# Two pairs of heads of batch 1, laid out crossed, share TensorE's 64x64 quadrants

## The chip, the core and the metric

The kernel runs on one core of one Trainium2 chip. A core has TensorE (PE in the profile; PEld is its loading of weights), VectorE (DVE), ScalarE (ACT), GpSimd (POOL, which here mostly issues DMAs) and SyncE (SP, which issues DMAs too). The metric is the device time of one launch in microseconds, the median of several runs.

## The reference

A sliding-window attention feeds a feed-forward layer with a squared ReLU. There are 8 batches, 8 heads, 576 tokens and 64 elements a head.

```python
scores = scale * np.matmul(q, k.transpose(0, 1, 3, 2))
rel = pos[:, None] - pos[None, :]
mask_plain = (rel >= 0) & (rel < window)
mask_dil = (rel >= 0) & (rel < window * dilation) & (rel % dilation == 0)
masks = np.stack([mask_plain if h < H // 2 else mask_dil for h in range(H)], axis=0)
...
attn = attn / (np.sum(attn, axis=-1, keepdims=True) + 1e-09)
return np.matmul(attn, v).astype(np.float32)
...
h = np.maximum(x @ w_in, 0.0)
return (h * h @ w_out).astype(np.float32)
```

The window is 32, the dilation 4. The first four heads ("plain") look at the last 32 tokens, the other four ("dilated") at every fourth of the last 128. The attention's output, 4608 tokens by 512, goes through w_in (512 by 2048) and w_out (2048 by 512).

## The kernel before, in words

**The feed-forward layer** makes up most of the work. It runs in tiles of 256 tokens (four of them) and then of 512. A tile is a list of groups, small closures of TensorE work: `mm1` multiplies by w_in (line 937 of the profile) into a PSUM tile `pf`, which ScalarE (line 950) and VectorE (line 951) turn into h2T, and `g2` multiplies by w_out (line 979), whose result ScalarE copies out (line 985).

**The attention** is put between these groups. Its heads come in pairs e = 0 to 3, of which 0 and 1 are plain, 2 and 3 dilated. The two heads of a pair (hl = 0, 1) lie in the lower and the upper 64 partitions. Batch 0 has code of its own, batches 0 and 1 are worked in two parts of 256 and 320 tokens, and from batch 2 on `quadrants` (line 661) runs products of 64x64 elements, four at a time, in the four quadrants of TensorE's array.

**Batch 1**, which the change touches, is laid out in block diagonals. K lies in `kbd`, a tile of 128x128 blocks with zeros off the diagonal, and V likewise in `vbd`. So one full 128x128 product does both heads of a pair, and half of the array multiplies by zeros. For a pair and a part the steps are:

- `trans` (line 277) transposes q or k on TensorE, and `halves` copies the result to `qT` or into the blocks of `kbd` (lines 297, 301, 308 and 314), on ScalarE or VectorE.
- `scores` (lines 351 and 357) multiplies keys by queries into a PSUM tile `pa`; ScalarE's exponential (line 361) and VectorE's mask (line 362) give the weights `pt`.
- `pv` multiplies V's blocks by the weights into a tile o (line 414), and a block diagonal of ones by them into a tile d (line 416), the denominators. Then ScalarE takes the logarithm of d (line 418) and the exponential of its negative (line 419), and VectorE multiplies o by that into `xT` (line 429), which is the feed-forward layer's input. The tiles o and d are `po` and `pd`, one buffer each, or two of the four buffers `pf` where the step's code ends in f.

**The order** is written out by hand in the string `PROGRAM`. Its fields, split at the bars, follow one group of the feed-forward layer each, and `step` runs each code: `1o0` is batch 1, `pv` of pair 0, first part; `1p2` is pair 2, second part; `1a3` are the scores of pair 3, first part, `1b0` those of pair 0, second part; q, Q, k and K transpose, and `2t0` and `2t1` do so for batch 2 with a copy out on ScalarE and VectorE (lines 264 and 262). All engines work off their queues in this order. The fields around the two places are

```python
"... | 1o2 | 1a0 1a1 | 1k3 1o0 1o1f | 1a3 1Q0 | 1K0 1o3 | 1Q1 1K1 | 1Q2 | 1b0 | ..."
"... | 1b2 1p0 | 1b1 1V3 1K3 | L3:x | 1p2 1p1f | 1b3 | 2t0 2t1 1p3f | ..."
```

**Crossed.** `crossed(b, e)` says for which pairs the keys of head hl meet the other half, so that head hl's scores come out in the other 64 partitions. Two pairs, one crossed and one not, then use different quadrants of the array. Before the change no pair of batch 1 is crossed. The code `n` in PROGRAM clears the off-diagonal halves of `kbd` ahead of batch 1 (lines 998 and 999). DMAs that load V (`load_v`, line 192, and line 219 for the last block) read from `crossed` which head goes where.

## Time and profile before

| what | value |
|---|---|
| median of 3 runs | 299.42 us (298.89 to 299.48) |
| the profiled execution | 299.32 us, span 297.5 us |
| TensorE busy | 290.4 us, 98% of the span, 3159 products |
| ScalarE, VectorE, GpSimd busy | 192.0, 168.0, 127.6 us |
| products with w_in, line 937 | 128.3 us, 704 |
| products with w_out, line 979 | 129.3 us, 592 |
| granted TensorE clock | 1.00 |

Times in the profile are microseconds from the start of the span. A row of the timeline has the start, the time, the engine, the line, the operation, out<-in, the form and the number of instructions merged in it; in brackets stands how long the engine was idle before, and what released it. A matmul's record runs to its modelled end, some 0.2 us for a small one, while the next one starts much earlier; the pace of products is therefore read from their starts, not from their durations. In a merged row with several widths, the form is that of the first. In the page, a line is followed by the share of the span in brackets and the number of instructions; the chain is that of the work that ended last.

### The profile page before, as it was taken

How to read it: one execution, taken by the hardware profiler on the slowest of the kernel's cores; microseconds unless marked ns; L12 is line 12 of the kernel's file. 1: busy time of each engine (PE TensorE's matmuls, PEld its weight loads, DVE VectorE, ACT ScalarE, POOL GpSimd, SP SyncE). 2: the span in 40 equal slices, each digit the busy share in tenths (PEclk: the TensorE clock that was granted, in tenths of full speed). 3: DMA queues.
4: the chain of work that ended last, by engine and by line, in shares of the span. 5: the costliest groups of instructions: out<-in, count | busy, mean ns of one | idle time of the engine just before them, and what ended most of it. 6: DMA issues, size and time to landing. Idle time of an engine off the chain costs nothing.

```text
span 297.5 us, 7852 instructions
## 1 busy us (share of the span) xinstructions
PE 290.4 (98%) x3159; PEld 166.3 (56%) x3159; DVE 168.0 (56%) x508; ACT 192.0 (65%) x397; POOL 127.6 (43%) x208
## 2 busy tenths in 40 slices
PE   7899999999999999999999999999999999999994
PEld 3589657868755554555455445545554555445443
DVE  2776566967868665686749474957445234004400
ACT  6888568757958665888667667766676567127411
POOL 8579882676584383955783688100000000000000
PEclk9999999999999999999999999999999999999999
DMA  8999999999989999999999499112101200121022
GB/s 126 197 183 215 203 157 223 186 151 169 193 114 185 184 121 190 153 125 175 159 191 151 65 160 186 13 37 73 35 2 36 74 35 0 35 73 35 0 56 88
DMA packets 83124, 35.37 MB, mean 119 GB/s; under 512 B 52624, under 2 KB 78480, under 8 KB 83088
## 3 DMA queue, kind: packets, MB, share of 16 engines
q0 software_dynamic: 48992, 18.40, 54.8%
q1 hardware_dynamic: 33952, 16.38, 27.7%
q8 instruction: 25, 0.41, 0.6%
q10 hardware_dynamic: 144, 0.10, 0.1%
q14 instruction: 11, 0.09, 0.1%
HBM read 37.31 MB, written 9.44 MB: 157 GB/s over the span
## 4 chain that ended last, share of the span: by engine, by line
PE 90%; DMA 5%; ACT 2%; POOL 1%; issue 1%; DVE 1%; ACTq 0%; POOLq 0%
PE pf L937 42%; PE pf L979 40%; DMA w_in<-in_moe_w_in_dram 3%; DMA kb<-in_k_dram 2%; PE po L661 2%; PE pa L661 1%; PE pf L661 1%; POOL qb L171 1%; PE pa L277 1%; PE pd L661 1%; ACT rec L684 0%; ACT pt L698 0%; POOL kb L171 0%; ACT rec L674 0%; PE po L414 0%
## 5 line engine op out<-in xcount | busy, mean ns | idle before, releaser
L937 PE MATMUL pf<-xT,w_in 128*128 128x512 bf16 (+1 forms) x704 | 128.3, 341 | 1.3 <-DMA w_in<-in_moe_w_in_dram 1.3
L979 PE MATMUL pf<-w_out_sb,h2T 128*128 128x512 bf16 (+2 forms) x592 | 129.3, 374 | 0.0
L937 PEld LDWEIGHTS <-w_in 128*128 128x128 bf16 x704 | 77.9, 113 | 48.0 <-DMA w_in<-in_moe_w_in_dram 1.7
L950 ACT ACTIVATE h2T<-pf 128x512 bf16<-128x512 f32 x144 | 83.7, 600 | 29.5 <-PE pf L937 29.3
L951 DVE TENSOR_TENSOR h2T<-h2T 128x512 bf16<-128x512 bf16 x144 | 60.3, 424 | 60.1 <-ACT h2T L950 57.8
L979 PEld LDWEIGHTS <-h2T 128*128 128x128 bf16 x592 | 55.5, 98 | 61.6
L478 POOL DMA_DIRECT2D vbd<-in_v_dram x80 | 43.0, 547 | 24.3 <-DMA qb<-in_q_dram 10.2
L985 ACT COPY osb<-pf 128x512 f32<-128x512 f32 (+1 forms) x34 | 19.5, 573 | 49.7 <-PE pf L979 49.5
L171 POOL DMA_DIRECT2D qb<-in_q_dram x18 | 13.0, 720 | 9.7 <-DMA xx<-qb 7.9
L684 ACT ACTIVATE rec<-rec 128x576 f32<-128x576 f32 x24 | 16.4, 682 | 0.7
L698 ACT ACTIVATE pt<-pa 128x384 bf16<-128x384 f32 (+1 forms) x28 | 12.7, 498 | 6.2 <-DVE xT L689 3.7
L192 POOL DMA_DIRECT2D vbd<-in_v_dram x16 | 10.9, 691 | 9.1 <-DMA kb<-in_k_dram 4.3
L687 DVE TENSOR_TENSOR xT<-po,rec 128x512 bf16<-128x512 f32 x14 | 9.7, 691 | 7.5 <-ACT rec L684 7.2
L171 POOL DMA_DIRECT2D kb<-in_k_dram x18 | 12.7, 706 | 1.7 <-issue 0.7
L465 POOL DMA_DIRECT2D vd<-in_v_dram x20 | 12.0, 616 | 2.9 <-DMA vbd<-in_v_dram 2.9
L470 POOL DMA_DIRECT2D vbd<-in_v_dram x20 | 12.0, 615 | 2.7 <-DMA vbd<-in_v_dram 2.2
L700 DVE TENSOR_TENSOR pt<-pt,mask_n 128x448 bf16<-128x448 bf16 (+1 forms) x20 | 7.1, 373 | 9.5 <-ACT pt L698 9.4
L700 DVE TENSOR_TENSOR pt<-pt,mask_f 128x384 bf16<-128x384 bf16 x24 | 8.4, 355 | 6.0 <-ACT pt L698 5.9
L687 DVE TENSOR_TENSOR xT<-pf,rec 128x512 bf16<-128x512 f32 x10 | 6.9, 691 | 8.5 <-ACT rec L684 8.5
L492 DVE COPY qT<-xx 64x576 bf16<-64x576 bf16 (+1 forms) x30 | 10.8, 360 | 0.6
L661 PEld LDWEIGHTS <-vbd 64*64 64x64 bf16 x288 | 7.6, 107 | 4.2 <-issue 4.2
L698 ACT ACTIVATE pt<-pf 128x448 bf16<-128x448 f32 (+1 forms) x18 | 8.5, 521 | 0.5 <-PE pf L661 0.3
(156 smaller groups left out, 311.8 us busy)
## 6 DMA issues: line engine op xcount, KB each, us to landing
qb<-in_q_dram POOLq DMA_DIRECT2D x7, 320.0 KB, 5.3
kb<-in_k_dram POOLq DMA_DIRECT2D x7, 320.0 KB
vd<-in_v_dram POOLq DMA_DIRECT2D x32, 64.0 KB, 6.1
w_in<-in_moe_w_in_dram POOLq DMA_DIRECT2D x4, 512.0 KB, 8.6
w_out_sb<-in_moe_w_out_dram POOLq DMA_DIRECT2D x4, 512.0 KB, 13.0
out_dram<-osb SPq DMA_DIRECT2D x16, 128.0 KB, 5.3
qb<-in_q_dram POOLq DMA_DIRECT2D x7, 256.0 KB, 7.6
kb<-in_k_dram POOLq DMA_DIRECT2D x7, 256.0 KB
```

The lines of the kernel that those rows point to most:

```text
L171: nc.gpsimd.dma_start(t[0:n, part, hs, :], src[b, hs, t0 : t0 + RES * n, :].rearrange("h (p r) d -> p h (r d)", r=RES))
L478: nc.gpsimd.dma_start(v_rows[b % 2][p0 + 16 * r : p0 + 16 * r + 16, e, :, :], v[b, 2 * e + hl, :, :].rearrange("(i m r) d -> r m i d", r=R ...
L661: nc.tensor.matmul(out, lhs, rhs, start=begin, stop=True, skip_group_check=True)
L684: nc.scalar.activation(rec[:, :], rec[:, :], ACT.Exp, scale=-1.0)
L687: nc.vector.tensor_tensor(out=tok[:, :, 16:M], in0=byr(o[:, :]), in1=byr(rec[:, 0:512]), op=ALU.mult)
L698: nc.scalar.activation(pt, sp[b, e][g][:, 0:n], ACT.Exp, scale=SCALE)
L700: nc.vector.tensor_tensor(out=pt, in0=pt, in1=mask, op=ALU.mult)
L937: nc.tensor.matmul(to, w_in_sb[piece][:, kt, c0 : c0 + 509 : 4], rhs, start=(kt == kts[0] and x == 0), stop=(kt == kts[-1] and x == per - ...
L950: nc.scalar.activation(hv, acc[u][:, :].rearrange("p (x n) -> p x n", x=per), ACT.Relu)
L951: nc.vector.tensor_tensor(out=hv, in0=hv, in1=hv, op=ALU.mult)
L979: nc.tensor.matmul(cur[m][:, c0:c1], h2[:, f, P * m : P * m + P], w_out_sb[:, f, c0:c1], start=(f == 0), stop=(f == NF - 1),)
L985: (nc.vector.tensor_copy if last and part == 1 or tk0 == 3 * NT // 2 else nc.scalar.copy)(osb[:, c0:c1], cur[m][:, c0:c1])
```

## The change

Pair 1 of batch 1 becomes crossed: `crossed` is now 1 for it, `halves` writes its keys into the anti-diagonal of `kbd`, `n` clears the diagonal of that pair's blocks and the off-diagonal of the others (six pieces instead of two), and `load_v` swaps its two heads. `pv` is split: `products` makes the lists of products, yields them, and goes on with logarithm, exponential and the multiplication. `pv` runs one pair as before. The new `pv_two` takes two pairs, cuts each product into the two 64x64 products on its blocks that aren't zero, and issues them in turn from four lists, one a quadrant. The steps `1o0 1o1f` become `1+o01`, and `1p2 1p1f` become `1+p21`. Pairs 0 and 3 in the second part, and 2 and 3 in the first, stay as they were.

The order on ScalarE, GpSimd and SyncE is the same as before, instruction for instruction. On VectorE the only difference are the four more pieces of clearing. On TensorE 16 products in the first place become 32, and 24 in the second become 48.

```diff
-    ... | 1k3 1o0 1o1f | 1a3 1Q0 | ... | 1p2 1p1f | 1b3 | ...
+    ... | 1k3 1+o01 | 1a3 1Q0 | ... | 1+p21 | 1b3 | ...
...
-        return int(b == XB and e in (1, 3) or b >= NATURAL and e == 1 or b >= PAIRED and e == 0)
+        return int(b == 1 and e == 1 or b == XB and e in (1, 3) or b >= NATURAL and e == 1 or b >= PAIRED and e == 0)
...
+            at = sides[hl ^ crossed(b, e)]
...
-                        kbd[rows, e, m0 // 16 : (m0 + n) // 16, rows].rearrange(
+                        kbd[rows, e, m0 // 16 : (m0 + n) // 16, at].rearrange(
...
+    def pv(*args):
+
+        work = products(*args)
+        mms, dms = next(work)
+        for y, items in enumerate((mms, dms)):
+            for x, (to, lhs, rh) in enumerate(items):
+                nc.tensor.matmul(to, lhs, rh, start=(x == 0), stop=(x == len(items) - 1), skip_group_check=True)
+        next(work, None)
+
+    def pv_two(b: int, one, two, part: int):
+
+        works = products(b, one, part), products(b, two, part, ps_f, "pf")
+        todo = {}
+        for e, work in zip((one, two), works):
+            for s, rows in enumerate(sides):
+                cols = sides[s ^ crossed(b, e)]
+                todo[s, cols.start] = items = []
+                lists = next(work) if s == 0 else lists
+                for kind in lists:
+                    for x, (to, lhs, rh) in enumerate(kind):
+                        items.append((to[cols], lhs[rows, rows], rh[rows], x == 0))
+        assert len(todo) == 4
+        while any(todo.values()):
+            for items in todo.values():
+                if items:
+                    to, lhs, rh, begin = items.pop(0)
+                    nc.tensor.matmul(to, lhs, rh, start=begin, stop=True, skip_group_check=True)
+        for work in works:
+            next(work, None)
...
-        for x, (oo, i, rh) in enumerate(mms):
-            nc.tensor.matmul(oo, vb[:, e, i, :], rh, start=(x == 0), stop=(x == len(mms) - 1), skip_group_check=True)
-        for x, (dd, rh) in enumerate(dms):
-            nc.tensor.matmul(dd, ones[:, :], rh, start=(x == 0), stop=(x == len(dms) - 1), skip_group_check=True)
+        yield [(oo, vb[:, e, i, :], rh) for oo, i, rh in mms], [(dd, ones[:, :], rh) for dd, rh in dms]
...
+        if code[0] == "+":
+            pv_two(b, int(code[2]), int(code[3]), int(code[1] == "p"))
+            return
...
-            zero_halves(kbd)
+            for es in (slice(0, 1), slice(2, NE)):
+                zero_halves(kbd[:, es])
+            for rows in sides:
+                nc.vector.memset(kbd[rows, 1, :, rows], 0.0)
```

## The prediction

> **What bounds the kernel now.** I read the page first: busy time of each engine, then the chain that ended last.

> ```profile
> PE 290.4 (98%) x3159; PEld 166.3 (56%) x3159; DVE 168.0 (56%) x508; ACT 192.0 (65%) x397; POOL 127.6 (43%) x208
> ...
> PE 90%; DMA 5%; ACT 2%; POOL 1%; issue 1%; DVE 1%; ACTq 0%; POOLq 0%
> ```

> TensorE is busy for 98% of the span and carries 90% of the chain, at full granted clock. So a product that gets shorter counts, but only if the engine then finds its next input ready. The edit touches batch 1 in two places, and next I read the timeline there, TensorE alone. First place, pairs 0 and 1, first part:

> ```profile
> 47.02 0.32 PE L414 MATMUL po<-pt,vbd 128*128 128x96 bf16 x4
> 47.17 0.32 PE L416 MATMUL pd<-pt,ones 128*128 128x96 bf16 x4
> 47.37 0.32 PE L414 MATMUL pf<-pt,vbd 128*128 128x96 bf16 x4
> 47.52 0.32 PE L416 MATMUL pf<-pt,ones 128*128 128x96 bf16 x4
> 47.68 0.38 PE L979 MATMUL pf<-w_out_sb,h2T 128*128 128x512 bf16 x1
> ```

> Each pair has eight products (three of 96 columns, one of 64, twice), starting 0.04 us apart: 0.31 us a pair. Both pairs start on a wait, which the busy share hides, since a matmul's record overlaps the next. The two masks of VectorE (line 362) run from 46.62 to 47.31 in that timeline, one after the other; pair 0 starts some 0.06 after the first ends, pair 1 at 47.37, 0.06 after the second.

> Second place, pair 2 (dilated) and pair 1, second part; no wait here, both masks are done by 63.92:

> ```profile
> 64.32 0.44 PE L414 MATMUL po<-pt,vbd 128*128 128x32 bf16 x9
> 64.59 0.38 PE L416 MATMUL pd<-pt,ones 128*128 128x320 bf16 x3
> 64.81 0.39 PE L414 MATMUL pf<-pt,vbd 128*128 128x32 bf16 x6
> 65.04 0.39 PE L416 MATMUL pf<-pt,ones 128*128 128x32 bf16 x6
> 65.26 0.38 PE L979 MATMUL pf<-w_out_sb,h2T 128*128 128x512 bf16 x1
> ```

> Behind the first place ScalarE, read alone, has no gap. What it does last here, line 361 at 48.99, is the exponential that pair 3 needs:

> ```profile
> 47.53 0.39 ACT L418 ACTIVATE rec<-pd 128x256 f32<-128x256 f32 x1 [0.58 <-PE pd L416]
> 47.94 0.42 ACT L419 ACTIVATE rec<-rec 128x256 f32<-128x256 f32 x1
> 48.27 0.37 ACT L418 ACTIVATE rec<-pf 128x256 f32<-128x256 f32 x1
> 48.66 0.42 ACT L419 ACTIVATE rec<-rec 128x256 f32<-128x256 f32 x1
> 48.99 0.36 ACT L361 ACTIVATE pt<-pa 128x256 bf16<-128x256 f32 x1
> ```

> Last I looked for 64x64 products elsewhere. Line 661 runs them from batch 2 on; these are its first and last rows at two visits:

> ```profile
> 83.21 0.38 PE L979 MATMUL pf<-w_out_sb,h2T 128*128 128x512 bf16 x1
> 83.52 0.23 PE L661 MATMUL po<-pt,vbd 64*64 64x96 bf16 x1
> ```
> ```profile
> 94.17 0.20 PE L661 MATMUL pa<-kbd 64*64 64x64 bf16 x2
> 94.30 0.41 PE L937 MATMUL pf<-xT,w_in 128*128 128x512 bf16 x1
> ```

> A 512-column product is followed by the next of its kind after 0.215 us; here the first quadrant starts 0.31 after it. So **going into quadrants costs 0.09 us**. Coming out, the last 64-column product (0.03) starts at 94.18 and the next full one at 94.30: **another 0.09**. Between, the visit from 83.52 to 84.22 holds 68 products, and four of 96 columns start every 0.04 us (two into po, two into pf: at 83.63, 83.67, 83.71). Four quadrants then really run beside each other, at the pace of one full product, though the first round takes 0.02 to 0.03 longer.

> **The change part by part.**

> *First place.* Removed: 16 full products. Added: 32 quadrant products in eight rounds of four (six of 96 columns, two of 64): 6 x 0.042 + 2 x 0.028 = 0.31 us for both pairs instead of 0.62. That would save 0.31, less 0.09 and 0.09 for the switches and 0.03 for the first round: 0.10. But the rounds mix the pairs, and TensorE issues in order. After the first two products of pair 0, pair 1's product waits for the second mask, until 47.37, and all of pair 0 now queues behind it; its head start of 0.35 is gone. The switch in hides in the first wait. So TensorE ends at 47.37 + 0.31 + 0.03 + 0.09 = 47.80 instead of 47.68: **0.12 later**.

> *What is late next.* The logarithm of pair 0 waits for its last denominator, which moves from the end of its own block into the last round: start about 47.66, record 0.19, handover 0.04, so 47.89 instead of 47.53, 0.36 later. ScalarE has no gap, so line 361 moves to 49.35, VectorE's mask behind it from 49.45 to 49.81. That mask is 0.28 long and now ends at 50.09; pair 3's product (at 49.81 before, by the timeline) starts 0.06 behind it, at 50.15: **0.34 later**, of which 0.12 is the above. The next wait in this chain is at 53.58, where the scores of pair 0's second part take a buffer that VectorE's copy (line 301, end 53.53) frees; it comes 0.36 later with ScalarE: **0.36 in all**. ScalarE is idle for 0.64 before 53.52 and the chain ends there; up to the second place all engines are later by this.

> *Second place.* Removed: 24 full products, 0.94 us. Added: 48 quadrant products in twelve rounds of uneven width (pair 2: 32, 80 four times, 64, then 320, 128, 64; pair 1: 32, 96 four times, 64, twice). With the durations of the old rows (32 columns 0.027, 64 0.028, 80 0.034, 96 0.042, 128 0.056, 320 0.134), pair 2's own quadrants need 0.49, and the slower of the two in every round adds up to 0.56; these are the bounds, and I take 0.53, since a short product lets its neighbour slip by a little. With 0.03 + 0.09 + 0.09 this is 0.74: **0.20 saved** (0.17 to 0.24). TensorE is now 0.16 late.

> *And late again.* Pair 2's last denominator also stands in the last round: 0.36 + 0.12 + 0.50 after 64.32, with its record 65.49, so the logarithm starts at 65.52 instead of 65.01, 0.51 later. ScalarE is without a gap to 67.27 (pair 3's exponential), VectorE from there to 70.25 by the timeline, and its last copy is this:

> ```profile
> 69.80 0.45 DVE L262 COPY qT<-pa 128x576 bf16<-128x576 bf16 x1
> ```

> It frees the buffer that the visit at 70.52 writes. It ends 0.27 before that visit and hands over in 0.05, so 0.22 of the 0.51 is slack: the visit starts **0.29 later**, more than the 0.16. Behind it TensorE is the bound again and its short waits (73.40, 84.76, 120.78) are for evictions and copies that it feeds itself, so they move along.

> *The other edits.* The zeroing of kbd on VectorE goes from two pieces of 1.02 us (34.38, 35.68) to six with the same elements. Four more starts cost between nothing and 0.28 each (the gap between the two), at most 1.1 us; VectorE is then idle for 2.74 us, until 39.43. Without that cover batch 1's first copies would be late by up to the 1.1. K's copies, V's loads and the scores keep their number and shape; only a column offset and the head read change, so 0. POOL's and SP's queues keep their order. V of pair 1 is wanted 0.03 earlier than before at most in the second place; the 40 extra weight loads run under the products, as in the visits.

> *Sum.* The profiled execution took 299.32 us (span 297.5, and 1.8 around it), 0.10 under the median of the runs shown, 299.42. Own time 299.32 + 0.29 = 299.61.

> **The rivals.**

> *Lateness of the masks does not count.* If pair 3 and the visit at 70.52 have more slack than I read, only TensorE's own terms are left: 0.12 - 0.20 = -0.08, or 299.24; if pair 1's wait were hidden as well, -0.10 - 0.20 = -0.30, or 299.02. For it: releasers are inferred. Against: 49.81 lies only 0.02 behind its mask's handover.

> *The rounds are slower, and the kernel with them.* In this order two row halves write one bank of po at once. If they took turns, the first place would last 0.31 more and the second 0.53; the logarithms move by as much, and the visit at 70.52 is 0.29 + 0.31 + 0.53 = 1.1 late: 300.45. It decides from 0.06 us a round on: 20 rounds of 0.018 more bring the sum past 0.6. Against it: the visit at 83.52 writes po from both halves with 0.04 a round. The change would then not do what it says. [...]

> *The lateness is carried on.* VectorE is 0.51 late at 70.25, and TensorE waits 0.34 for it at 84.76 already. If nothing between takes that up, the end moves by 0.51: 299.83.

> **How the numbers follow.** A measurement of this kernel tells about 0.2%, 0.6 us, from no change. Forecast 0.58, at 299.6, 0.08% up and so no change; masks without effect 0.13 (299.0 to 299.2); carried on 0.14 (299.8); slow rounds 0.10 (300.4); a wait elsewhere that I don't see 0.05, slower. The shown runs spread from 298.89 to 299.48, so I let 0.04 of the cases below end beyond 0.2% faster, and 0.09 of the forecast and the carried case beyond 0.2% slower: faster 0.04, same 0.72, slower 0.24. The range runs from the first rival's 299.1 to 300.3, short of the full slow rounds.

> **What would show it.** In the changed kernel: pair 0 and 1 in 64x64 rows, two of them near 47.02 and the rest from 47.37 on; the next line 979 near 47.80; the logarithm near 47.9; pair 3's product near 50.15; the second place about 0.74 long; the visit now at 70.52 about 0.3 later, and the same shift at the end. Rounds much over 0.04, a first place that ends before 47.68, or pair 3 at its old time would make me wrong.

## The result, and the profile after

The changed kernel takes **300.83 us** (median of 22 runs), the kernel before 299.60 us (median of 22 runs beside it). The ratio is **1.0048, 95% interval 1.003 to 1.0066**: 0.5% slower, and 0.2% can be told from no change. Single runs of the changed kernel lie between 299.8 and 302.9 us, but for one, many near 300 and many near 302, and those of before mostly between 299.0 and 300.5. That spread is part of what has to be explained. The profiled execution took 301.07 us, span 299.3. The new functions move the lines: 937 is now 968, 979 is 1010, 661 is 692, 418 and 419 are 446 and 447, 301 is 302, 361 is 362, 503 is 534; full products of batch 1 are line 374, those in quadrants line 394.

The page of the changed kernel, busy time, instruction queue and chain (28 records of products are missing from this trace; all 3199 weight loads are there):

```profile
PE 289.5 (97%) x3171; PEld 166.1 (56%) x3199; DVE 168.0 (56%) x512; ACT 192.1 (64%) x397; POOL 129.1 (43%) x208
...
q8 instruction: 25, 0.41, 0.6%
...
PE 92%; ACT 3%; issue 2%; DVE 2%; ACTq 0%
```

TensorE's busy time is about the same, as far as the missing records let one see, and the span is 1.8 longer: it stands still more. I compare places by the start of the same instruction in both traces. This run is 0.17 us late before it reaches the first place; other runs, with and without the edit, are up to 0.34 early or 0.21 late there at full clock, so it is taken off below as the run's own.

First place, timeline of TensorE in the changed kernel:

```profile
47.20 0.23 PE L394 MATMUL po<-pt,vbd 64*64 64x96 bf16 x2
47.55 0.23 PE L394 MATMUL pf<-pt,vbd 64*64 64x96 bf16 x2
47.56 0.23 PE L394 MATMUL po<-pt,vbd 64*64 64x96 bf16 x2
47.59 0.23 PE L394 MATMUL pf<-pt,vbd 64*64 64x96 bf16 x2
...
47.83 0.19 PE L394 MATMUL pd<-pt,ones 64*64 64x64 bf16 x2
```

Two quadrant products run, then all wait 0.35 us for pair 1's mask, and from 47.55 the rounds of four come some 0.04 us apart, two row halves of `po` beside each other. (By the starts of weight loads, the next full product follows at 48.00; its own record is missing.) ScalarE and pair 3's product behind it, two views of the same kernel:

```profile
48.10 0.39 ACT L446 ACTIVATE rec<-pd 128x256 f32<-128x256 f32 x1 [0.98 <-PE pf L394]
```
```profile
50.36 0.28 PE L374 MATMUL po<-pt,vbd 128*128 128x64 bf16 x4
```

The logarithm starts at 48.10 instead of 47.53, which less 0.17 is 0.40 later, and pair 3's product starts at 50.36 instead of 49.81, which less 0.17 is 0.37 to 0.38 later. Second place, and the visit behind it:

```profile
64.99 0.20 PE L394 MATMUL po<-pt,vbd 64*64 64x32 bf16 x2
...
65.50 0.19 PE L394 MATMUL pd<-pt,ones 64*64 64x64 bf16 x2
```
```profile
65.62 0.55 PEld L1010 LDWEIGHTS <-h2T 128*128 128x128 bf16 x4
```
```profile
70.90 0.30 PE L692 MATMUL pa<-xx 64*64 64x80 bf16 x6
```

The visit's first product is at 70.90 instead of 70.52, 0.2 later after taking off the 0.17; by 71 us TensorE is 0.27 late, again without the 0.17. So far the sum of the prediction holds. What it lacks stands in the weight loads of the stretch behind, with the idle time before each row in brackets:

```profile
75.60 2.08 PEld L968 LDWEIGHTS <-w_in 128*128 128x128 bf16 x19 [0.45 <-issue]
79.08 1.44 PEld L1010 LDWEIGHTS <-h2T 128*128 128x128 bf16 x8
82.03 2.06 PEld L1010 LDWEIGHTS <-h2T 128*128 128x128 bf16 x11 [1.51 <-DVE xT L720]
```

Two halts, before 75.60 and before 82.03, and no wait explains them. "issue" says that nothing is known to release the first. For the second the profile names a multiplication of VectorE, but that is only its inference: the product multiplies h2T, of which the last piece was written by 79.16, and in the second trace of the same kernel (experiment 6) it starts at 80.08, while that multiplication ends at 81.34. By comparing starts, TensorE is 0.44 late before the first halt, 0.89 behind it and 2.07 behind the second (the halt is 1.39 long in the weight loads; the products around it start at 80.64 and 82.04, 1.40 apart instead of the usual 0.22, so 1.18 is lost). The wait for line 503 at 84.76 then takes up 0.37, and **1.71** stays; at the end it is 1.75. In the kernel before the same stretch has one row without a halt:

```profile
78.20 4.89 PEld L979 LDWEIGHTS <-h2T 128*128 128x128 bf16 x24
```

The two halts have one thing in common. If one counts TensorE's instructions in the order of its program, they stand at numbers 1986 and 2242, which is **exactly 256 apart**. Queue q8, of the kind "instruction", shows 25 packets, 0.41 MB, so 16 KB each (16384 bytes by the trace), for some 6460 instructions of TensorE, one for 256 of them.

**Theory 1, fetch,** my guess from these counts: TensorE's program comes in blocks of 256 instructions, and the fetch of the next one starts only when a block has been used up. A dense stretch of quadrants would then use up a block sooner than the next one arrives. The change adds 40 weight loads and 40 products ahead of that stretch (and drops four waits for semaphores, so 76 instructions in all) and so moves all block ends into another place. **Theory 2, chain:** the late logarithms and copies that I worked out are worth more than I thought, somewhere further on. **Theory 3, layout:** the crossed layout itself costs something.

### The profile page after: what moved, and what is told of

The parts are those of the page before. It is cut to its first block, busy times and chain, and to the rows that moved or that the text cites. A ratio compares the mean times of both kernels' runs of the same rounds, so it can differ in the third digit from the quotient of the medians.

```text
span 299.3 us, 7904 instructions
## 1 busy us (share of the span) xinstructions
PE 289.5 (97%) x3171; PEld 166.1 (56%) x3199; DVE 168.0 (56%) x512; ACT 192.1 (64%) x397; POOL 129.1 (43%) x208
## 4 chain that ended last, share of the span: by engine, by line
PE 92%; ACT 3%; issue 2%; DVE 2%; ACTq 0%
PE pf L968 41%; PE pf L1010 39%; PE po L762 2%; PE po L692 2%; PE pf L692 1%; PE pa L692 1%; PE pa L792 1%; PE pd L692 1%; PE pf L844 1%; ACT h2T L981 1%; DVE xT L915 1%; ACT rec L905 1%; PE pa L277 1%; ACT rec L446 0%; ACT rec L908 0%
## 5 line engine op out<-in xcount | busy, mean ns | idle before, releaser
L1010 PE MATMUL pf<-w_out_sb,h2T 128*128 128x512 bf16 (+2 forms) x571 | 127.4, 373 | 2.6 <-DVE xT L720 1.0
L509 POOL DMA_DIRECT2D vbd<-in_v_dram x80 | 44.1, 567 | 20.8 <-DMA kb<-in_k_dram 7.8
L192 POOL DMA_DIRECT2D vbd<-in_v_dram x16 | 10.9, 690 | 8.1 <-DMA kb<-in_k_dram 3.3
L501 POOL DMA_DIRECT2D vbd<-in_v_dram x20 | 12.1, 624 | 0.4 <-issue 0.4
```

The lines of the kernel that those rows point to most:

```text
L509: nc.gpsimd.dma_start(v_rows[b % 2][p0 + 16 * r : p0 + 16 * r + 16, e, :, :], v[b, 2 * e + hl, :, :].rearrange("(i m r) d -> r m i d", r=R ...
L1010: nc.tensor.matmul(cur[m][:, c0:c1], h2[:, f, P * m : P * m + P], w_out_sb[:, f, c0:c1], start=(f == 0), stop=(f == NF - 1),)
```

## The experiments

**1. Shift the blocks without the change.** Warming products at the start, `w10` (ten, which in the kernel before start some 0.43 us apart up to 3.60 us and 0.21 to 0.22 apart from 3.95 on), are replaced by more and smaller ones, so that TensorE's program is longer ahead of everything. For N = 43 after w5 this is 76 instructions more, for 18 after w8 it is 32.

```diff
-    "... L1:q10123 w10 T00 ..."
+    "... L1:q10123 w5 &43 T00 ..."
...
+        elif code[0] == "&":
+            turn(int(code[1:]), 64)
```

> The kernel before, with five of the ten 512-column products that warm TensorE up at the start replaced by 43 small ones of 64 columns: 76 instructions more on TensorE ahead of everything, nothing else. Fetch theory (TensorE's instructions come in blocks of 256, and a block that is used up in less than about 6.5 us leaves it waiting): every block now ends 38 products earlier than before; by the starts in the trace of before, the 256 instructions that end near 79.3 us then take 4.8 us, so a pause of 1 to 2 us there that no semaphore explains, and 1.0 to 2.0 us more on the whole. Chain theory (late masks, logarithms and copies after the two places are worth more than I worked out): no place is changed, so no more than 0.3 us.

> The control for the small products: the same edit with two of the ten replaced by 18, 32 instructions more on TensorE. Fetch theory: by the trace of before, blocks that end 16 products earlier take 6.56 us at the least, as much as the 6.5 that before shows without a pause, so within 0.3 us of before. Chain theory: the same.

Measured: with 76 more instructions 301.08 us beside 299.58, ratio 1.0047 (1.0018 to 1.0077), about as much as the change itself; with 32 more 299.47, ratio 0.9996 (0.998 to 1.0012). No work of batch 1 was touched, so a loss of this size needs neither quadrants nor a crossed layout. That halts make it is not shown by this run: the traced execution (299.35 us) was the shortest of its 12, with a halt of only 0.25 us at the place named, where 1 to 2 was expected; the others go up to 305.0.

**2. One place at a time.** The step of one place is put back to `1o0 1o1f` or `1p2 1p1f`, with everything else of the change kept.

```diff
-    "... | 1+p21 | ..."
+    "... | 1p2 1p1f | ..."
```

> The change with quadrants in the first place alone; in the second, pairs 2 and 1 run as full products (pair 1 is laid out crossed, so its two heads come out exchanged there, which costs no time). 32 instructions more instead of 80. Fetch theory: no block gets much shorter than 6.5 us, so no pause, and the lateness of the chain is all there is: 0.36 us more by my working, 0.2 to 0.5. Chain theory: the 1.2 us of the change stem from the first place, so 0.8 to 1.5 more.

> The change with quadrants in the second place alone; in the first, pairs 0 and 1 run as full products (two heads exchanged there). 48 instructions more. Fetch theory: no block gets much shorter than 6.5 us; TensorE saves 0.2 and the logarithm of pair 2 is 0.15 late, within its slack, so 0.0 to 0.2 us less than before; the sum of the two single places is then well below the 1.2 us of both. Chain theory: what the first place does not explain of the 1.2 us shows here, so first and second alone add up to it.

Measured: quadrants in the first place alone 300.24, ratio 1.0022 (1.0005 to 1.004); in the second alone 299.30, ratio 0.9993 (0.9973 to 1.0013). Their sum is 0.15%, against 0.5% for both together, though the intervals are wide enough that this alone would not settle it. Neither trace has a halt at a block's end in the stretch. In the trace of the first place alone TensorE comes out of the chain 0.38 us later than it went in, in that of the second alone 0.20 earlier, as in the whole change. Together with experiment 1 it speaks for theory 1.

**3. Worse and better shifts.** The same edit, now 144 instructions more in the kernel before, and 48 and 112 more in the changed one.

> The kernel before, with nine of the ten warming products replaced by 81 small ones: 144 instructions more on TensorE ahead of everything. Fetch theory: by the starts in the trace of before, the 256 instructions that now end near 70.8 us take 4.0 us, the shortest block of all shifts, and two more take 6.2 to 6.6; with a need of 5.3 to 6.9 us a block (what the pauses seen so far give) TensorE pauses 1.3 to 2.9 us at the end of that block, whatever it waits for otherwise, and the kernel takes 1.3 to 3 us more. Chain theory: no more than 0.3 us.

> The changed kernel, with three of the ten warming products replaced by 27 small ones: 48 instructions more ahead of everything. Fetch theory: by the trace of the changed kernel, less its two pauses, the 256 instructions that end near 72.3 us now take 4.5 us, those that end near 78.3 us 6.0; so the pause moves from about 80 to about 72 us, lasts 0.8 to 2.4 us, and the kernel takes 1.2 to 3 us more than before, somewhat more than the change itself (1.2). Chain theory: the same as the change, 1.2, and its pauses stay where they were.

> The changed kernel, with six of the ten warming products replaced by 62 small ones: 112 instructions more ahead of everything. Fetch theory: by the same reckoning the shortest blocks now take 5.7 us (near 71.1) and 6.35 (near 84) instead of 5.0, so the pause near 80 us is gone, and what is left of them is 0 to 1.2 us near 71; 0.4 to 1.3 us more than before, of which 0.3 to 0.4 is the chain. Chain theory: 1.2 as for the change.

Measured: 144 more in the kernel before, 300.49, ratio 1.0041 (1.0028 to 1.0054); 48 more in the changed kernel, 300.78, ratio 1.0065 (1.0039 to 1.0091); **112 more in the changed kernel, 299.96, ratio 1.0012 (0.9992 to 1.0032)**. Adding instructions to the changed kernel took most of its loss away. Where the halts went, by the weight loads of the first and the second of these kernels:

```profile
71.03 0.12 PEld L661 LDWEIGHTS <-kbd 64*64 64x64 bf16 x3
72.20 0.10 PEld L661 LDWEIGHTS <-kbd 64*64 64x64 bf16 x1 [1.05 <-issue]
```
```profile
76.09 1.31 PEld L968 LDWEIGHTS <-w_in 128*128 128x128 bf16 x12 [2.13 <-issue]
```

In the first, TensorE halts for 1.05 us in the midst of a visit's quadrants, between two loads of the same kind; in the second for 2.13 us, at the block end that was named, and the halt near 80 us is gone. (This execution took 303.25 us; another 1.8 us of its lateness arose before 25 us, where TensorE's granted clock was 0.50 from 8 to 10 us.) In the third there is 0.13 us left at the place named. The miss: I expected 1.3 to 3 us of 144 instructions, and it was 1.2 (0.8 to 1.6), since the next block came 5.2 us after the one before, sooner than the 5.3 to 6.9 that I had allowed.

**4. The fetch by itself.** 400 small products in one run, at two places of the kernel before.

```diff
         group()
+        if g in (len(groups) * 2 // 5, len(groups) * 7 // 8):
+            first.pop("W", None)
+            turn(400, 64)
```

> The disputed cost by itself: the kernel before, with 400 small products of 64 columns put in one run behind a group of the feed-forward layer at two fifths of its groups (the DMA queues are busy) and again at seven eighths (they are nearly idle); the time as such says nothing. Fetch theory: 128 products of 0.03 to 0.045 us are 4 to 6 us, so at the busy place the run halts at every 256th instruction, such that blocks come 5.3 to 7 us apart; at the idle place the fetch is shorter, and the blocks come 3.5 to 5 us apart, with shorter halts or none. Chain theory, or if instructions are not fetched in such blocks: an even run at both places.

```profile
138.37 7.78 PEld L731 LDWEIGHTS <-kbd 128*128 128x128 bf16 x264 [1.45 <-issue]
147.19 3.79 PEld L731 LDWEIGHTS <-kbd 128*128 128x128 bf16 x128 [1.04 <-issue]
151.19 0.26 PEld L731 LDWEIGHTS <-kbd 128*128 128x128 bf16 x7 [0.21 <-issue]
```
```profile
278.16 11.92 PEld L731 LDWEIGHTS <-kbd 128*128 128x128 bf16 x400
```

These weight loads wait for no data. The 1.45 us ahead of the first row is another wait: it lies 16 instructions ahead of a block's end, and the first product waits for a semaphore there. Two block ends lie within the row of 264 loads, at 138.60 and 142.36, and pass without a halt, the second of them against what was expected. At the next two the run halts, for 1.04 and 0.21 us, and between these halts stand exactly 128 loads, with their products 256 instructions. At the second place the same 400 run evenly, 0.029 us apart, 3.73 us a block. The queues' share of 16 engines' time, in 142 to 152 us and in 278 to 290 us of this kernel:

```profile
q1 hardware_dynamic: 4247, 1.05, 67.6%
q0 software_dynamic: 1285, 0.15, 26.8%
q8 instruction: 2, 0.03, 1.4%
```
```profile
q1 hardware_dynamic: 160, 0.26, 7.4%
q8 instruction: 3, 0.05, 1.8%
```

So the next block was there sooner at the idle place, after 3.73 us or less with q1 at 7.4%. At the busy place, with q1 and q0 at 94% together, blocks came 3.8, 4.8 and 4.0 us apart, less than the 5.3 to 7 that I expected; the load there is also lower than the 177% of 75 to 80 us in the changed kernel. For the whole program q8 now shows 31 packets for some 7980 instructions, again one for 256.

**5. Less to move.** GpSimd is held up ahead of its loads of batch 3's V.

```diff
-    "... | L3:Vd0 L4:q00123 L4:q10123 "
+    "... | %28 L3:Vd0 L4:q00123 L4:q10123 "
...
+        elif code[0] == "%":
+            for _ in range(int(code[1:])):
+                nc.gpsimd.memset(scrap[:, :], 0.0)
```

> The changed kernel, with GpSimd held up ahead of its loads of batch 3's V (which it issues from 71.9 us on) by 28 small memsets of a spare tile, some 7 to 9 us by the duration of the memsets in the trace; the loads follow about 8 us later, TensorE's instructions and their order are untouched. Fetch theory, with the fetch slowed by the load on the DMA engines: with less to move between 72 and 80 us the blocks of instructions arrive sooner, both pauses shrink to 0.5 us or less together, and the kernel comes back to 0.3 to 0.6 us over before. If blocks take as long whatever the DMA engines carry, the pauses stay and so does the 1.2. If V now comes too late for the visit near 94 us, a wait for it shows there and the time says nothing.

> The control: the same memsets in the kernel before. Both theories: within 0.3 us of before, since it shows no such pause; if the delay itself costs something, it is seen here.

Measured: 307.27 and 307.59 us, ratios 1.0246 (1.02 to 1.0292) and 1.0254 (1.0221 to 1.0287). The times say nothing, as was feared, only at another place: the memsets took 10.5 us, and a visit waited 5.5 us at 116.7, in the control 4.9. The trace says something. Queue shares from 75 to 80 us (packets overlap, so they can add up to more than 100%), first the changed kernel, then this one:

```profile
q1 hardware_dynamic: 2458, 0.61, 106.6%
q0 software_dynamic: 1048, 0.29, 70.6%
```
```profile
q1 hardware_dynamic: 2946, 0.73, 118.6%
q0 software_dynamic: 326, 0.04, 12.0%
```

GpSimd's queue q0 fell from 71% to 12%, and the second halt from 1.39 to 0.02 us, with TensorE's instructions unchanged. The first halt stayed, 0.44 us; its fetch was under way at 71.6, before the memsets began at 72.3. By itself this run shows little: the second trace of the changed kernel (experiment 6) has no halt there either, with q0 at 56% and q1 at 84% from 74 to 79 us. Experiment 4 is what speaks for the load.

**6. The layout alone, and the change once more.** Full products in both places, with the crossed layout kept:

```diff
-    "1+o01 | ... | 1+p21 | ..."
+    "1o0 1o1f | ... | 1p2 1p1f | ..."
```

> The crossed layout alone: pair 1's keys and V crossed and the six pieces of clearing, but full products in both places (the two heads of pair 1 come out exchanged). TensorE's instructions are those of before, one for one. Fetch theory: the same as before within 0.3 us, no pause. A theory by which the layout (copies, clearing, loads) carries part of the 1.2 us: 0.4 or more.

> The changed kernel once more, for a second trace of it. Fetch theory: if TensorE pauses, it is at the same two weight loads, the first of the instructions 1986 and 2242 of its program, for 0 to 2.5 us in sum; the end is later than before by the pauses and 0.1 to 0.4 us, and a run with small pauses is at 299.8 to 300.2. A theory with another cause: the pauses lie elsewhere, or the time differs without them.

Measured: the layout alone 300.04 beside 299.70, ratio 1.001 (0.9984 to 1.0036), so no difference that can be told; theory 3 explains at most a part. The change once more 301.59, ratio 1.0051 (1.0022 to 1.008), single runs from 299.5 to 303.8. This time the traced execution was a short one, 299.95 us, and it is the piece that was missing. Its weight loads in the same stretch:

```profile
73.63 3.39 PEld L968 LDWEIGHTS <-w_in 128*128 128x128 bf16 x31 [0.19 <-issue]
78.47 4.52 PEld L1010 LDWEIGHTS <-h2T 128*128 128x128 bf16 x22
```

The same kernel, and no halt. At 80.8 us it is 0.33 later than before; the execution with halts was 2.07 later there. So the two traces of one kernel, 299.95 and 301.07 us, differ by the halts, less what the wait at 84.76 takes up, and by 0.25 us that arose before 25 us.

**All blocks together.** Read from the trace's records of queue q8 and of the weight loads, times in us, each from the start of the block that is being used:

```
kernel        block    its 256      fetch    fetch   next     halt
              starts   instr. take  starts   takes   starts
before        68.81    8.34         3.60     1.27    8.34     -
before        77.15    6.57         2.54     1.06    6.57     -
changed       68.29    6.86         4.20     1.50    7.31     0.45
changed       75.60    5.04         3.78     0.88    6.43     1.39
again         68.04    6.90         2.83     0.88    6.90     -
again         74.94    5.15         2.00     0.89    5.15     -
b_pad38       74.60    5.04         2.87     1.08    5.29     0.25
b_pad72       67.04    4.10         2.77     0.89    5.16     1.06
a_pad24       69.50    4.47         3.81     1.27    6.60     2.13
a_pad56       65.40    5.71         3.56     0.93    5.83     0.13
a_quiet       75.66    5.04         2.64     0.96    5.06     0.02
dense, busy  142.36    3.73         2.20     1.13    4.83     1.10
dense, idle  281.85    3.73         0.46     1.12    3.73     -
```

At every halt of the table TensorE goes on 1.3 to 1.8 us after the fetch has landed; in its rows without a halt the fetch had landed 2.1 us or more before the block's end. (At 142.36 in the run of experiment 4 it had landed 1.5 us before, and no halt is seen.) The packet itself takes 0.88 to 1.50 us in the table, 1.92 at 84.59 in the kernel before, once 2.7, ahead of the first halt of a_quiet. What varies more is how long it takes to start: 0.5 to 1.0 us on idle DMA engines (experiment 4, second place), 1.7 to 4.2 us at the halts, and by up to 1.8 us from run to run at the same place (3.78 and 2.00 in the two traces of the changed kernel). That can be the spread of its single runs.

**A halt in the kernel before.** The same count finds one that was there all along. Seven blocks ahead of the second halt's instruction stands the first weight load of the feed-forward layer, and the kernel before has this:

```profile
15.02 1.68 PEld L937 LDWEIGHTS <-w_in 128*128 128x128 bf16 x16 [1.33 <-DMA w_in<-in_moe_w_in_dram]
```

The profile names a DMA of w_in. But in all nine traces in which this load is the first instruction of a block, it waits 0.7 to 1.5 us and starts 1.34 to 1.49 us after a packet of q8 has landed, wherever that falls between 13.3 and 14.3 us. In the five traces of shifted kernels, where no block ends there, the same load waits 0.2 us or less. The halt costs little, since the next loads then wait for w_in instead: at 25 us the two shifted kernels before with full clock are 0.11 us earlier and 0.20 later than before.

What is not shown: the profile has no event that says "waits for instructions", so theory 1 rests on the place of the halts, on the shifts and on the records of q8. Which of the untraced runs halted, and for how long, can't be seen. A lower clock is not what sets most of the long runs apart: of the changed kernel's 33 runs between 299.5 and 303.9 us in its two series, 15 are above 301.5, and 13 of these have a granted clock of 0.999 or 1.00. It is a second source of spread, though: the traced execution with 32 more instructions took 303.24 us, has no halt at a block's end, and was 3.7 us late by 17 us, after a granted clock of 0.50 from 8 us on.

## Why the prediction was wrong

I predicted 299.6 (299.1 to 300.3) and no change that can be told. It is 300.83, slower. By its steps:

*First place, 0.12 later.* Right: 0.15. The queueing behind pair 1's mask, the round of 0.04 and the switches came as worked out.

*Pair 3's product 0.34 later, 0.36 in all.* Right: 0.37 to 0.38, and 0.40 at the next wait (54.16 instead of 53.58, less 0.17).

*Second place 0.20 saved.* Right: from 64.99 to the next product of line 1010, whose weights are loaded at 65.62 and which starts some 0.02 behind, it lasts 0.65 where 0.94 stood. Of the 0.29 the switch in, 0.09 and ahead of 64.99, has to be taken off. *Visit at 70.52 0.29 later.* Nearly: its first product 0.20, and TensorE behind it 0.27, 0.30 in the second trace, each less the lateness that its run had ahead of the first place.

*Slow rounds.* Did not come: rounds of 0.04 us, with two row halves of `po` beside each other. No run shows the halves taking turns, on which the 300.4 rested.

*"Behind it TensorE is the bound again and its short waits (73.40, 84.76, 120.78) are for evictions and copies that it feeds itself, so they move along."* Wrong for 84.76. Line 503 copies keys that a DMA has transposed, so that wait does not follow TensorE. It is 0.30 in before, 0.57 in the layout alone, 0.62 in the second trace of the change, and it shrank from there to nothing in the one with halts. It gave 0.37 back in that trace and cost 0.3 in the other. This is the rest of the difference between my 299.61 and the 299.95 of the execution without halts.

*"the 40 extra weight loads run under the products, as in the visits"*, costed at nothing. **This is the step that failed.** Their time on the array is hidden, in rounds of 0.04 us, but each weight load and each product is an instruction, and 80 more of them (76 with the waits that fell away) moved the ends of the blocks behind: 6.57 us for one block became 5.04 in the densest stretch, where the next one came 6.43 us after the one before in this trace, and after 5.15 or less in the second. That cost 0.45 and 1.39 us in the traced execution, 1.64 of it net, and 1.3 after the wait at 84.76. I had it only as "a wait elsewhere that I don't see", at a chance of 0.05, and without a mechanism: I never counted instructions, nor looked at queue q8, whose 0.6% of the DMA engines' time looked like nothing.

Theory 2 stands as the small part: quadrants in the first place alone cost 0.22% (0.05 to 0.40), where I had 0.36 us, 0.12%; and with its block ends shifted by 112 instructions the whole change costs 0.12% (-0.08 to 0.32), 0.36 us, which is near to the 0.29 that I worked out. Even so nothing here is faster than before beyond the measurement: the best, quadrants in the second place alone, is at 0.9993.

## What to carry to other kernels

Splitting a product on the diagonal into its two quadrants doubled its instructions on TensorE here (16 products became 32, 24 became 48, with a weight load each), so beside the time on the array count the instructions: mark every 256th in the traced program, which is one packet of q8 here. In this case halts that no wait explains came behind blocks that took 3.7 to 6.9 us while the DMA queues were busy, and the runs spread (299.8 to 302.9 us); not every such block had one (5.15 us, in the second trace of the change, had none). To tell such a halt from a data wait, shift the program by a few dozen harmless instructions at its start: here 48 more took the halt near 80 us away and left one of 2.13 us at another block's end. Make this shift once or twice before an edit is judged by its time, since otherwise the phase of its blocks is measured with it: the same change read 1.0048, and 1.0012 with 112 instructions more.
